# A decode-attention backward kernel: ordering the heads by batch, so that one batch's serial chain runs under the other batch's heads

## The chip, the cores and the metric

One core of one Trainium2 chip. The metric is the device time of one execution in microseconds (us); lower is better.

## The reference

A transformer block for one new token per batch (B = 2) with adaptive layer norm: attention over a cache of 8192 keys and values (32 heads of width 128), then a gated MLP. What is asked for is the output and all the gradients of its inputs. Cut to what matters:

```python
def _A_ref(x, k_cache, v_cache, wq, wo):
    q = (x @ wq).reshape(B, Sq, H, Dh).transpose(0, 2, 1, 3)
    scores = jnp.einsum('bhqd,bhkd->bhqk', q, k_cache) * Dh ** (-0.5)
    p = _softmax(scores, axis=-1)
    o = jnp.einsum('bhqk,bhkd->bhqd', p, v_cache)
    return o.transpose(0, 2, 1, 3).reshape(B, Sq, H * Dh) @ wo
...
    x = x + ga * _A_ref(h, A_k_cache, A_v_cache, A_wq, A_wo)
    h = _layernorm(x, axis=-1) * (1 + cb) + sb
    x = x + gb * _B_ref(h, B_w1, B_w3, B_w2)
...
_out, _vjp = jax.vjp(_f, A_x, A_k_cache, A_v_cache, ...)     # gradients of all of these
```

K, V, dK and dV are 134 MB each; everything else is small. Each of the 64 (batch, head) pairs has 2 MB of K and of V. The gradients dV = p dO and dK = ds q need dO, and dO comes from the end of the block back through the MLP and `wo`. So there is a serial chain between the two passes over the heads: O, attention projection, norm, MLP forward, MLP backward, norm backward, dO. **That chain mixes heads but not batches**: batch 0's chain needs the heads of batch 0 only.

## The kernel before

It has three parts, one after the other. Heads alternate between the batches. Time is cut into *slots*, eight to a head; in a slot of stage A TensorE does 8 transposes of K blocks, 8 score matmuls and 16 matmuls for M (a 128 x 128 product of V and weighted K, needed for dq) and for one more column.

```python
    def hb(i):
        return i % B, i // B                 # batch, head: the batches alternate
    ...
    def load(store, src, i):                 # 2 MB of K or V into one of ten "big" tiles
    ...
    # stage A: scores, softmax, M; 64 heads
    for t in range(NSLOT + MOFF + 1):
        i, g = divmod(t, NG)
        ...
        kts[(i, g)] = transposes(K[i], g, g in (2, 6))
        ...
                nc.tensor.matmul(S_ps[si][:, cc:cc + 1], kt[:, j, :], qT_bf[:, h, b:b + 1], ...)
        ...
            mm_m(mi, mg)                     # 16 matmuls, N = 129 and N = 1
            if mg == NG - 1:
                if mi < NHD - KEEPV: V.pop(mi)          # the last two V heads are kept
                if mi + 4 < NHD:     load(K, A_k_cache, mi + 4)
                if mi + 3 < NHD:     load(V, A_v_cache, mi + 3)
                if mi == min(2, NHD - 5): load_wo()
                if mi == NHD - 3:         load_ffn()
    # the middle: one long dependent sequence for both batches, with the weights
    # transposed on TensorE for the backward products
    ...
        for h in range(H):
            nc.tensor.matmul(av[:, dc, :], wo_v[h // (H // 2)][:, h % (H // 2), dc * P:(dc + 1) * P],
                             O_bf[:, h, :], start=(h == 0), stop=(h == H - 1))
    for a in range(2):
        for h0 in range(0, H, 4):
            t_wo(a, h0)                      # transposes of wo; later of w2, w1, w3
    ...                                      # MLP forward and backward, dO
    # stage C: V again, dV and dK; 64 heads; small outputs as "tasks" in between
    for t in range(NSLOT + LAG + 2 * NQ + 4):
        ...
            kts[(n, g)] = transposes(V[order[n]], g, g in (2, 6))
        ...
            ev_dv(n, g // 2)                 # VectorE outer product, 128 x 2048, into a big tile; 1 MB stores
        ...
            ev_dk(u // NG, (u % NG) // 2)
```

Of the kernel before, what the change touches and what calls it, by code (L numbers as in the profile page):

```python
# [18 lines left out]
def kernel(  # L19
# [48 lines left out]
    NBIG = 10  # L68
# [4 lines left out]
    def hb(i):  # L73
        return i % B, i // B
# [8 lines left out]
    ktp = ctx.enter_context(tc.tile_pool(name="ktp", bufs=5))  # L83
# [6 lines left out]
    def big():  # L90
        return bigp.tile([P, BIG], BF16, name="big", tag="big")

# [15 lines left out]
    E2 = cst.tile([P, NHD, KK, 2], BF16, name="E2")  # L108
# [31 lines left out]
    V = {}  # L140

    def load(store, src, i):
        b, h = hb(i)
        t = big()
        v = t[:, 0:KK * P].rearrange("p (k d) -> p k d", k=KK)
        qd.dma_start(v, src[b, h].rearrange("(p kk) d -> p kk d", p=P))
        store[i] = v
# [10 lines left out]
    load(K, A_k_cache, 0)  # L158
    load_wq(1)
    load(K, A_k_cache, 1)  # L160
    load_wq(2)
    load_wq(3)
    for a in range(2):
        qd.dma_start(wm_v[a][:, :, M1:MD], wm_d[:, 2 * a:2 * a + 2, M1:MD])
    load(V, A_v_cache, 0)
    load(K, A_k_cache, 2)
    load(V, A_v_cache, 1)
    load(K, A_k_cache, 3)
# [114 lines left out]
    evac_n = [0]  # L283

    def evac(dst, src):
        if evac_n[0] % 2 == 0:
            nc.scalar.copy(dst, src)
        else:
            nc.vector.tensor_copy(dst, src)
        evac_n[0] += 1  # L290

    S_ps = {}
    M_ps = {}
    ek = {}
    kts = {}
    M_t = {}
    MOFF = NG + LAG + 5
    NSLOT = NHD * NG

    def pair(ap, n):  # L300
        return ap.rearrange("p k (a b) -> p k a b", b=2)

    def transposes(src, g, dve):
        tp = tps.tile([P, GRP, P], BF16, name="tp", tag="tp")
        for j in range(GRP):
            nc.tensor.transpose(tp[:, j, :], src[:, g * GRP + j, :], identb[:])  # L306
        kt = ktp.tile([P, GRP, P], BF16, name="kt", tag="kt")
        if dve:
            nc.vector.tensor_copy(kt[:], tp[:])  # L309
        else:  # L310
            nc.scalar.copy(kt[:], tp[:])  # L311
        return kt

    def chain_rowmax(i):
        rm = hw.tile([P, 1], BF16, name="rm", tag="rm")
        nc.vector.tensor_reduce(rm[:], S_ps[i][:, 0:KK], AX.X, ALU.max)
        kts[("rm", i)] = rm

    def chain_b(i):
        s = S_ps[i]  # L320
        nc.tensor.matmul(s[:, P:2 * P], kts.pop(("rm", i))[:].to_broadcast((P, P)), nident[:],  # L321
                         start=True, stop=True)
        nm = hw.tile([P, 1], F32, name="nm", tag="nm")
        nc.vector.tensor_reduce(nm[:], s[:, P:2 * P], AX.X, ALU.min)  # L324
        kts[("nm", i)] = nm

    def chain_e(i):
        s = S_ps.pop(i)
        nc.scalar.activation(E2[:, i, :, :], s[:, 0:KK].unsqueeze(2).to_broadcast((P, KK, 2)), ACT.Exp,  # L329
                             bias=kts.pop(("nm", i))[:], scale=SCL, accum_out=rsum[:, i:i + 1])  # L330

    def scale_k(i, q):
        t = ekp.tile([P, QK, 130], BF16, name="ek", tag="ek")
        ks = slice(q * QK, (q + 1) * QK)
        nc.vector.tensor_tensor(pair(t[:, :, 0:P], QK), pair(K[i][:, ks, :], QK),  # L335
                                E2[:, i, ks, :].unsqueeze(2).to_broadcast((P, QK, P // 2, 2)), ALU.mult)
        nc.gpsimd.tensor_copy(t[:, :, P:P + 1], E2[:, i, ks, 0:1])  # L337
        ek[(i, q)] = t

    def mm_m(i, g):  # L340
# [3 lines left out]
        t = ek[(i, g // 2)]  # L344
        for j in range(GRP):
            kk = g * GRP + j
            nc.tensor.matmul(m[:, 0:P + 1], V[i][:, kk, :], t[:, kk % QK, 0:P + 1],  # L347
                             start=(kk == 0), stop=(kk == KK - 1), skip_group_check=True)
            nc.tensor.matmul(m[:, P + 1:P + 2], K[i][:, kk, :], E2[:, i, kk, 0:1],  # L349
                             start=False, stop=(kk == KK - 1), skip_group_check=True)  # L350
        if g == NG - 1:
            K.pop(i)

    def m_evac(i):
        m = M_ps.pop(i)
        nc.scalar.copy(M_all[:, i, :], m[:, 0:P])  # L356
        nc.vector.tensor_copy(OK[:, i, :], m[:, P:P + 2])  # L357

    KEEPV = 2
    extra = {}  # L360

    def at(slot, f):
        extra.setdefault(slot, []).append(f)

    for pc in range(1, NPC):
        at(2 * pc, lambda pc=pc: q_part(pc))
    at(NG, lambda: mod_part(2 * NC, MC))
# [3 lines left out]
    def load_wo():  # L371
        for a in range(2):
            t = big()
            v = t[:, 0:H // 2 * D].rearrange("p (h d) -> p h d", d=D)
            qd.dma_start(v, A_wo.rearrange("(h p) d -> p h d", p=P)[:, a * (H // 2):(a + 1) * (H // 2), :])
            wo_v.append(v)

    wn = {}
    nfull = F // P

    def load_ffn():
        for nm, ap in (("w1", B_w1), ("w3", B_w3)):
            t = big()
            wn[nm] = t[:, 0:NC * F].rearrange("p (k f) -> p k f", k=NC)
            qd.dma_start(wn[nm], ap.rearrange("(k p) f -> p k f", p=P))
        t = big()
        wn["w2"] = t[:, 0:FC * D].rearrange("p (k d) -> p k d", k=FC)
        qd.dma_start(wn["w2"][:, :nfull, :], B_w2[0:nfull * P].rearrange("(k p) d -> p k d", p=P))
        if FL != P:
            qd.dma_start(wn["w2"][:FL, nfull, :], B_w2[nfull * P:F])  # L390

    M_all = None
    Mt = None
    for t in range(NSLOT + MOFF + 1):
        i, g = divmod(t, NG)
        u = t - (NG + LAG + 2)
        if u >= 0 and u % NG == 0 and u // NG < NHD:
            chain_e(u // NG)
        if i < NHD:
            if g == 0:  # L400
                S_ps[i] = stps()
            kts[(i, g)] = transposes(K[i], g, g in (2, 6))
        for f in extra.pop(t, []):
            f()
        s = t - LAG
        if 0 <= s < NSLOT:
            si, sg = divmod(s, NG)
            b, h = hb(si)
            kt = kts.pop((si, sg))
            for j in range(GRP):  # L410
                cc = sg * GRP + j
                nc.tensor.matmul(S_ps[si][:, cc:cc + 1], kt[:, j, :], qT_bf[:, h, b:b + 1],  # L412
                                 start=True, stop=True)
        for off, f in ((0, chain_rowmax), (1, chain_b)):
            u = t - (NG + LAG + off)
            if u >= 0 and u % NG == 0 and u // NG < NHD:
                f(u // NG)
        u = t - (NG + LAG + 3)
        if u >= 0 and u % 2 == 0 and u // NG < NHD:
            scale_k(u // NG, (u % NG) // 2)  # L420
        u = t - MOFF
        if 0 <= u < NSLOT:
            mi, mg = divmod(u, NG)
            mm_m(mi, mg)
            if mg == NG - 1:
                if mi < NHD - KEEPV:
                    V.pop(mi)
                if mi + 4 < NHD:
                    load(K, A_k_cache, mi + 4)
                if mi + 3 < NHD:  # L430
                    load(V, A_v_cache, mi + 3)
                if mi == min(2, NHD - 5):
                    load_wo()
                if mi == NHD - 3:
                    load_ffn()
        if t == NG:
            load(V, A_v_cache, 2)
        u = t - MOFF - 1
        if u >= 0 and u % NG == NG - 1:
            if M_all is None:  # L440
                Mt = big()
                M_all = Mt[:, 0:NHD * P].rearrange("p (i d) -> p i d", d=P)
            m_evac(u // NG)

    woT = [big(), big()]
    woT_v = [t[:, 0:2 * HD].rearrange("p (k m) -> p k m", k=2) for t in woT]

    def tgroup(blocks, dsts):
        tp = tps.tile([P, GRP, P], BF16, name="tp", tag="tp")
        flat = tp[:].rearrange("p a b -> p (a b)")  # L450
        for o, n, src, rows in blocks:
            nc.tensor.transpose(flat[:n, o:o + rows], src, identb[:rows, :rows])
        for dst, (n, o, w, k) in dsts:
            s = flat[:n, o:o + w]
            if k > 1:
                s = s.rearrange("p (k m) -> p k m", k=k)
            evac(dst, s)

    def t_wo(a, h0):
        nh = min(4, H - h0)  # L460
        blocks = []
        for d2 in range(2):
            for hh in range(nh):
                h = h0 + hh
                src = wo_v[h // (H // 2)][:, h % (H // 2), (2 * a + d2) * P:(2 * a + d2 + 1) * P]
                blocks.append(((d2 * nh + hh) * P, P, src, P))
        tgroup(blocks, [(woT_v[a][:, :, h0 * P:(h0 + nh) * P], (P, 0, 2 * nh * P, 2))])

    tot = mtps()
    nc.tensor.matmul(tot[:, 0:NHD], onesf[:], rsum[:], start=True, stop=True)  # L470
    rtot = col("rtot", H)
    rtot_f = rtot[:].rearrange("p h b -> p (h b)")
    nc.vector.tensor_scalar(rtot_f, tot[:, 0:NHD], 0.5, None, ALU.mult)
    nc.vector.reciprocal(rtot_f, rtot_f)
    O32 = col("O32", H)
    O32_f = O32[:].rearrange("p h b -> p (h b)")
# [528 lines left out]
```

## Time and profile before

1856.85 us was the median of four runs (1851.69 to 1862.42). The profiled execution has a span of 1847.5 us.

| stage | from, us | to, us | what binds it |
|---|---|---|---|
| A | 40 | 768 (last M matmul) | TensorE |
| middle | 768 | 822 (first dV store issued) | the dependent sequence; no large transfer |
| C | 822 | 1823 (last store issued) | DMA |

First the part of the profile's page that shows the span in 40 slices of 46 us. Digits are tenths of a slice in which the engine was busy; PEclk is the TensorE clock granted, in tenths of full speed.

```profile
PE   5889999999999999888868776676555555555560
PEclk9999999999999999976555558576766565656665
DMA  9998999999999999449999999999999999999996
GB/s 389 412 374 326 383 394 380 388 379 380 380 372 367 371 361 361 186 179 387 415 411 420 416 415 423 418 418 417 421 419 417 418 418 417 416 415 413 416 415 254
```

The hole is at slices 17 and 18. Left of it, from slice 5 on, DMA moves 361 to 394 GB/s; right of it, from slice 20 to the last but one, 411 to 423: stage A could take more bytes, stage C could not. Busy time by stretches says why. The columns are the stretch and its length, busy time and count for five engines, the granted clock, the DMA engines' busy share and GB/s.

```profile
core 0: us, PE busy (x) PEld busy (x) DVE busy (x) ACT busy (x) POOL busy (x), PEclk, DMA share, GB/s
185.00:277.00 92.00, 89.52 (x2167) 88.63 (x2164) 54.72 (x77) 55.62 (x77) 16.48 (x33) 1.00 0.98 389
462.00:554.00 92.00, 86.28 (x2084) 85.43 (x2082) 52.34 (x75) 53.17 (x73) 19.07 (x32) 1.00 0.94 376
760.00:780.00 20.00, 18.28 (x418) 18.02 (x415) 10.83 (x18) 6.04 (x10) 3.15 (x4) 0.91 0.30 104
780.00:800.00 20.00, 13.76 (x279) 13.25 (x277) 8.13 (x35) 9.38 (x15) 0.00 (x0) 0.74 0.01 2
900.00:1000.00 100.00, 76.52 (x782) 57.11 (x780) 62.74 (x71) 53.45 (x81) 21.23 (x38) 0.50 1.01 413
```

TensorE is busy 97% of the first of these stretches of A and 94% of the second, at full clock. In C the clock is halved for most of the time (0.50 from 900 to 1000 us) and nobody minds, because DMA's share is 1.01. The ends of the hole come from the first and last start of one line's instructions: the M matmul, and the store of a dV or dK half.

```profile
L347 PE MATMUL m_ps<-ek,big x4096: 217/217/269, 43.7 to 767.9; 128*128 128x129 bf16 x196
L903 POOL DMA_DIRECT2D out_dram<-big x256: 531/531/676, 822.1 to 1823.3; - x128
```

### The profile page before, as it was taken

The numbers are of one execution on the slowest core, as the hardware profiler recorded it, in microseconds if no ns is written. First come the engines' busy times: TensorE is split into PE (matmuls) and PEld (weight loads), VectorE is DVE, ScalarE is ACT, GpSimd is POOL, SyncE is SP. The second block draws the span as 40 slices with busy tenths as digits, with TensorE's granted clock in tenths as the row PEclk, the third lists the DMA queues.
The fourth block names the chain that finished last, engine by engine and source line by source line (L and its number), as shares of the span: only waits on it lengthen the run. The fifth ranks groups of instructions, "written<-read, shape, count | busy, mean of one in ns | idle before, by whom it ended". The sixth has DMA issues, their size and how long they took to land. (4 is left out here: it accounts for less than half of the span.)

```text
span 1847.5 us, 58876 instructions
## 1 busy us (share of the span) xinstructions
PE 1387.5 (75%) x26588; PEld 1293.8 (70%) x26588; DVE 1132.5 (61%) x1415; ACT 955.3 (52%) x1244; POOL 303.9 (16%) x557
## 2 busy tenths in 40 slices
PE   5889999999999999888868776676555555555560
PEld 5889999999999998876556565575455555555550
DVE  2545565655555555547656666677687666666682
ACT  3545565565555555447546566474444444444440
POOL 0111111222222211102211111211111111111111
PEclk9999999999999999976555558576766565656665
DMA  9998999999999999449999999999999999999996
GB/s 389 412 374 326 383 394 380 388 379 380 380 372 367 371 361 361 186 179 387 415 411 420 416 415 423 418 418 417 421 419 417 418 418 417 416 415 413 416 415 254
DMA packets 79784, 709.57 MB, mean 384 GB/s; under 512 B 8160, under 2 KB 13644, under 8 KB 21932
## 3 DMA queue, kind: packets, MB, share of 16 engines
q1 hardware_dynamic: 38304, 421.57, 56.9%
q0 software_dynamic: 41216, 284.22, 37.0%
q8 instruction: 208, 3.41, 0.7%
q14 instruction: 44, 0.36, 0.0%
q10 hardware_dynamic: 12, 0.01, 0.0%
HBM read 421.57 MB, written 284.20 MB: 382 GB/s over the span
## 5 line engine op out<-in xcount | busy, mean ns | idle before, releaser
L311 ACT COPY kt<-tp 128x1024 bf16<-128x1024 bf16 x768 | 776.3, 1014 | 677.5 <-PE tp L306 667.9
L306 PE MATMUL tp<-identb,big 128*128 128x128 bf16 x8192 | 798.6, 256 | 26.3 <-issue 14.5
L306 PEld LDWEIGHTS <-big 128*128 128x128 bf16 x8192 | 601.2, 115 | 118.7 <-issue 111.4
L347 PE MATMUL m_ps<-ek,big 128*128 128x129 bf16 x4096 | 409.9, 218 | 10.4 <-issue 10.0
L958 PE MATMUL s_ps<-DO_bf,kt 128*128 128x1 bf16 x4096 | 196.4, 169 | 263.5 <-DVE kt L309 262.3
L958 PEld LDWEIGHTS <-kt 128*128 128x128 bf16 x4096 | 192.9, 111 | 282.6 <-DVE kt L309 280.9
L349 PE MATMUL m_ps<-E,big 128*128 128x1 bf16 x4096 | 381.5, 165 | 9.1 <-issue 8.6
L895 DVE TENSOR_TENSOR big<-QD,E 128x2048 bf16<-128x2048 bf16 x256 | 311.4, 1217 | 117.0 <-DMA out_dram<-big 67.5
L895 DVE TENSOR_TENSOR big<-QD,ds 128x2048 bf16<-128x2048 bf16 x256 | 311.8, 1219 | 95.4 <-PE tp L306 62.8
L309 DVE COPY kt<-tp 128x1024 bf16<-128x1024 bf16 x256 | 176.1, 688 | 300.4 <-PE tp L306 256.3
L347 PEld LDWEIGHTS <-big 128*128 128x128 bf16 x4096 | 345.0, 96 | 10.7 <-issue 10.0
L349 PEld LDWEIGHTS <-big 128*128 128x128 bf16 x4096 | 343.4, 96 | 11.7 <-issue 11.4
L335 DVE TENSOR_TENSOR ek<-big,E 128x2048 bf16<-128x2048 bf16 x256 | 306.5, 1218 | 2.5 <-ACT E L329 2.2
L903 POOL DMA_DIRECT2D out_dram<-big x256 | 136.3, 532 | 831.8 <-DVE big L895 355.8
L337 POOL COPY ek<-E 128x16 bf16<-128x16 bf16 x256 | 143.7, 563 | 619.9 <-ACT E L329 272.3
L412 PE MATMUL s_ps<-qT_bf,kt 128*128 128x1 bf16 x4096 | 177.9, 164 | 14.5 <-issue 11.3
L412 PEld LDWEIGHTS <-kt 128*128 128x128 bf16 x4096 | 158.3, 97 | 18.8 <-issue 14.3
L710 ACT CAST stg<-m_ps 128x512 bf16<-128x512 f32 (+2 forms) x123 | 71.5, 591 | 106.2 <-DMA out_dram<-stg 69.8
L709 PE MATMUL m_ps<-big 2*128 2x512 bf16 (+2 forms) x123 | 71.2, 579 | 33.4 <-ACT stg L710 32.7
L324 DVE TENSOR_REDUCE nm<-s_ps 128x1 f32<-128x128 f32 x64 | 18.6, 291 | 58.4 <-PE s_ps L321 58.4
L357 DVE COPY OK<-m_ps 128x2 f32<-128x2 f32 x64 | 10.2, 159 | 55.4 <-ACT big L356 55.4
L814 ACT COPY kt<-tp 128x1024 bf16<-128x1024 bf16 x28 | 28.7, 1044 | 3.5 <-PE tp L811 3.3
(198 smaller groups left out, 481.9 us busy)
## 6 DMA issues: line engine op xcount, KB each, us to landing
out_dram<-big POOLq DMA_DIRECT2D x256, 1024.0 KB, 29.5
big<-in_A_v_cache_dram SPq DMA_DIRECT2D x126, 2048.0 KB, 13.3
big<-in_A_k_cache_dram SPq DMA_DIRECT2D x64, 2048.0 KB, 8.7
out_dram<-stg POOLq DMA_DIRECT2D x22, 512.0 KB, 19.5
big<-in_A_wq_dram SPq DMA_DIRECT2D x8, 512.0 KB, 14.5
big<-in_A_wo_dram SPq DMA_DIRECT2D x2, 2048.0 KB, 17.8
big<-in_A_wq_dram SPq DMA_DIRECT2D x2, 2048.0 KB, 15.2
big<-in_w_mod_dram SPq DMA_DIRECT2D x2, 1536.0 KB
```

Source lines behind the costliest of these rows:

```text
L306: nc.tensor.transpose(tp[:, j, :], src[:, g * GRP + j, :], identb[:])
L309: nc.vector.tensor_copy(kt[:], tp[:])
L311: nc.scalar.copy(kt[:], tp[:])
L335: nc.vector.tensor_tensor(pair(t[:, :, 0:P], QK), pair(K[i][:, ks, :], QK), E2[:, i, ks, :].unsqueeze(2).to_broadcast((P, QK, P // 2, 2)), ...
L337: nc.gpsimd.tensor_copy(t[:, :, P:P + 1], E2[:, i, ks, 0:1])
L347: nc.tensor.matmul(m[:, 0:P + 1], V[i][:, kk, :], t[:, kk % QK, 0:P + 1], start=(kk == 0), stop=(kk == KK - 1), skip_group_check=True)
L349: nc.tensor.matmul(m[:, P + 1:P + 2], K[i][:, kk, :], E2[:, i, kk, 0:1], start=False, stop=(kk == KK - 1), skip_group_check=True)
L412: nc.tensor.matmul(S_ps[si][:, cc:cc + 1], kt[:, j, :], qT_bf[:, h, b:b + 1], start=True, stop=True)
L710: nc.scalar.copy(st["t"][:lw, o:o + rw], ps[:lw, 0:rw])
L895: nc.vector.tensor_tensor(pair(dst[:, ks, :], QK), QD[n][:, which, :].rearrange("p (a b) -> p a b", b=2).unsqueeze(1).to_broadcast((P, QK, ...
L903: sq_.dma_start(dst_dram[b, h].rearrange("(p kk) d -> p kk d", p=P)[:, ks, :], t[:, ks, :])
L958: nc.tensor.matmul(DP[sn][:, cc:cc + 1], kt[:, j, :], DO_bf[:, h, b:b + 1], start=True, stop=True)
```

## The change

Its intent: heads are ordered batch by batch. Batch 0's chain is cut into small steps of one or two slots each, 165 slots in all, and laid between the slots of stage A of batch 1; batch 1's chain is laid in stage C of batch 0; C starts at slot 518, before A's last M (slot 526). So that a chain's steps are small, the backward products no longer transpose the weights on TensorE: a vector is spread over the partitions, and VectorE takes dot products of it with the rows of the weights. The chains hold `wo`, `w1`, `w3`, `w2` in four of the big tiles for most of the time, so the buffers are cut anew: seven big tiles and seven halves instead of ten big ones; K and the outputs use halves; the exponentials are stored once, not in pairs; no V head is kept from A to C (4.2 MB more to read). And there are 70 padding matmuls at slot 320. The diff, cut to its core:

```diff
-    NBIG = 10
+    NBIG = 7
+    NHALF = 7
...
     def hb(i):
-        return i % B, i // B
+        return i // H, i % H
...
+    def dot(acc, w, vec):
+        n = w.shape[-1]
+        r = w.shape[0]
+        junk = tps.tile([P, GRP * P // 2], F32, name="junk", tag="tp")
+        nc.vector.scalar_tensor_tensor(junk[:r, 0:n], w, 1.0, vec, ALU.mult, ALU.mult,
+                                       accum_out=acc)
...
+        def attn_pe(dc):
+            hold[dc] = scr(1)
+            for h in range(H):
+                nc.tensor.matmul(hold[dc], wo_v[h // (H // 2)][:, h % (H // 2), dc * P:(dc + 1) * P],
+                                 O_bf[:, b, h:h + 1], start=(h == 0), stop=(h == H - 1))
...
+    CS0 = end_a(sA[H - 1]) + 1
+    FS0 = max(NG + 4, CS0 - 2 * length(dh[0]))
+    want(FS0 - 2, "big", 1, lambda: load_ffn(0))
+    want(FS0 - 1, "big", 1, lambda: load_ffn(1))
+    t0 = lay(dh[0], FS0)
+    t0 = lay(dh[1], t0 + 1)
+    t0 = max(CS0, t0 + 1)
+    want(t0 - 2, "big", 1, lambda: load_wo(0))
+    want(t0 - 1, "big", 1, lambda: load_wo(1))
+    t0 = lay(ch[0], t0)
+    TC = max(NG * NHD + 6, t0 + 1)
+    CS1 = end_a(sA[NHD - 1]) + 1
+
+    def pad_pe():
+        d = scr(1)
+        for _ in range(70):
+            nc.tensor.matmul(d, identb[:], identb[:, 0:1], start=True, stop=True)
+
+    at(320, PL_X, pad_pe)
+    t1 = lay(ch[1], max(CS1, t0 + 1))
+    sC = [TC + NG * n for n in range(H)]
...                                 # removed: the middle, with its 260 weight transposes
```

`want(slot, ...)` queues a load in the order of the slot in which its data is needed; `lay` puts a chain's steps into slots.

## The prediction

> **What bounds the kernel now**, read from busy time by stretches and instruction groups by line.
> - Stage A (40 to 768 us, scores and M for 64 heads) is TensorE's: PE is busy 96% between 185 and 554 us at a granted clock of 1.00, while DMA moves about 380 GB/s. DMA showed 423 GB/s at 45 to 85 us, when reads really bind, so A has some 10% of DMA in hand. A head takes 10.95 us early, 11.4 late.
> - The middle (attention projection, MLP forward and backward, dO) is serial. The last M matmul starts at 768 us, the first dV product at 818, its store is issued at 822. The slices there show 186 and 179 GB/s; from 755 to 845 us about 15.5 MB move where 417 GB/s would move 37.5: some 53 us of DMA are lost.
> - Stage C (822 us to the end) is DMA's: share 1.01, 413 to 419 GB/s, 6.29 MB and so 15.1 us a head. The chain of waits ends in stores. Trainium skill, "DMA: Bandwidth & Descriptors", "Where 436 GB/s comes from": the ports' ceiling is 435 GB/s; the trace's 417 to 425 agrees, so C itself can't get faster.
>
> **What the change does.** It orders heads by batch. Batch 0's chain runs inside A of batch 1, batch 1's inside C of batch 0; C starts at slot 518, before A's last M (slot 526). Weight transposes (260 matmuls, 20 us busy) and their 34 evictions become about 78 DVE dot products per batch.
> - Removed: nearly the whole hole. First dV store moves from 822 to about 779 us.
> - Added to A: about 260 thin matmuls of batch 0 (128 took 3.5 us, so 7 us), 34 spreads (2 us), 70 padding matmuls (2 us), small waits: 12 to 17 us, on the critical path, since PE binds. The wo load leaves the start, where PE lost some 18 us, but wo and MLP weights (8.4 MB, 20 us of DMA) now come in mid A, with V down to two buffers: about even.
> - Added to C: two V heads are no longer kept, 4.2 MB or 10 us. DVE: a head needs 8 products of 1.22, two copies of 0.69 and one of 0.34 us, 11.5 us; a 512-wide dot is estimated at 0.69 us (from the 128-wide reduction at 0.29 and 64-wide vector operations at 0.225), 67 over 20 heads, plus small steps: 14.2 of 15.1 us. Tight; about 5 us of DMA may leak.
>
> Sum on the profile: 779 + 1001 (C as before, first to last store issue) + 10 + 5 + 22 us of drain = 1817; less loss in A brings about 1808. Against 1847.5 that is -1.6 to -2.1%. Predicted time **1815 us**, range 1785 to 1846. Chances: faster by over 2% 0.54, within 2% 0.43, slower 0.03.
>
> **What would show it.** The two slices near 180 GB/s are gone, none below 300 between first and last; the first dV store issues at 770 to 785 us; A stays PE-bound at 96%; C stays at DMA share 1.0 and 410 to 418 GB/s; traffic 714 MB; DVE busy over 85% while batch 1's chain runs.
>
> **What would make it wrong.** (1) Slower: with two V buffers and blocked-at-the-head loads, A starves around slots 216 to 290 and PE idles long enough to drop its clock (Trainium skill, "TensorE: Matmul & The Clock Gate", "The HAM clock gate": idle windows halve the clock; the trace shows 0.66-0.71 after such gaps at 135 and 165 us). (2) DVE becomes C's limit while batch 1's chain runs: DMA below 400 GB/s there. (3) Faster: A's thin matmuls fit into its issue gaps, and the early PE loss vanishes: A ends by 770, total about 1795.

## The result

1832.46 us, median of 11 runs (1822.54 to 1835.92), against 1854.62 us for the kernel before (15 runs, 1846.14 to 1862.42). Ratios are the mean time of one kernel's runs over that of the other's of the same rounds, so not quite the ratio of the medians. Here it is 0.9869, 95% interval 0.9849 to 0.9889: 1.3% faster, clear of noise, and less than 2%. The profiled execution has a span of 1824.1 us.

The slices after:

```profile
PE   5988999898999999986555657776868667455463
PEclk9999999998999999976565556555565856666676
DMA  9988999999889999999999999999999999999997
GB/s 387 374 318 347 383 376 402 408 371 331 354 349 379 383 371 374 370 355 391 421 418 421 423 423 412 422 408 407 409 415 414 423 415 411 422 418 402 415 412 315
```

The hole has gone. But slices 10 to 12 have sunk to 331 to 354 GB/s, which they did not before. The ends of the stages, from the same two kinds of line:

```profile
L434 PE MATMUL m_ps<-ek,big x4096: 217/217/272, 43.7 to 795.3; 128*128 128x129 bf16 x196
L909 POOL DMA_DIRECT2D out_dram<-half x256: 531/531/676, 788.0 to 1808.8; - x128
```

| | before | after | difference |
|---|---|---|---|
| first store issued | 822.1 | 788.0 | -34.1 |
| first to last store issued | 1001.2 | 1020.8 | +19.6 |
| last store issued to the end | 24.2 | 15.3 | -8.9 |
| span | 1847.5 | 1824.1 | -23.4 |

A's last M comes 27.4 us later than before. Where those went is read from the steps of the heads. I take the start of each head's second reduction of the softmax maximum, one per head, which stands in both kernels. Heads are counted from 0, in us:

| | head 25 | head 40 | head 63 | heads 25 to 40 | a head after 40 |
|---|---|---|---|---|---|
| before | 330.6 | 497.1 | 759.9 | 166.5 | 11.43 |
| after | 325.6 | 523.0 | 780.6 | 197.4 | 11.20 |

The changed kernel is 5 us ahead at head 25, loses 31 us up to head 40, where batch 0's chain and its weights come in, and is a little faster per head after that: at head 63 it is 21 us behind. The other 7 us come between that head and the last M, where C's first slots are already mixed in. Within heads 25 to 40, heads 32 to 36 take 61.5 us against 45.3. Busy time in 2-us stretches shows the worst of it:

```profile
426.00:428.00 2.00, 1.48 (x35) 1.35 (x34) 1.12 (x2) 1.32 (x3) 0.00 (x0) 1.00 1.07 440
428.00:430.00 2.00, 0.00 (x1) 0.01 (x1) 1.90 (x6) 0.05 (x1) 0.37 (x2) 1.00 1.02 426
430.00:432.00 2.00, 2.00 (x59) 2.00 (x60) 0.39 (x1) 1.01 (x1) 0.26 (x1) 0.92 0.98 414
432.00:434.00 2.00, 2.00 (x39) 2.00 (x37) 0.16 (x1) 0.75 (x1) 0.00 (x0) 0.50 0.99 414
438.00:440.00 2.00, 2.00 (x39) 2.00 (x37) 0.07 (x1) 0.78 (x1) 0.18 (x1) 0.50 0.94 250
444.00:446.00 2.00, 2.00 (x38) 2.00 (x37) 0.58 (x5) 1.01 (x1) 0.22 (x1) 0.67 0.98 414
446.00:448.00 2.00, 2.00 (x52) 2.00 (x49) 0.82 (x2) 0.15 (x1) 0.00 (x0) 1.00 0.32 127
```

TensorE stops at 428; the list of waits in 425 to 432 us names K:

```profile
PE tp L373 <- DMA half<-in_A_k_cache_dram: 2.5, 1, 2.5
```

Then the granted clock (third number from the right) is 0.50 from 432 to about 445 us, and the number of matmuls in 2 us falls from 52-60 to 39. The K was late because the two halves of `wo` (4 MB) had been queued ahead of it at 406 us. At the same place 128 thin matmuls (one moving column each) of the attention projection are inserted, 32 to a slot. A page of the Trainium skill, "TensorE: Matmul & The Clock Gate", section "The HAM clock gate", says that an idle window of about 3.4 us halves the clock; here 2.5 us without a matmul (0.52 us before 428 and the 2 us after it) and the thin stretch after it were enough. Which of the two did it the trace alone does not say. It is also not the only dip: between heads 25 and 40 the clock is 0.50 for 27 us in all, from 342.9 to 349.7 us after another late K (2.3 us), from 418.0 to 421.4 after a stop of 1.7 us with no wait behind it, and from 506.8 to 510.2.

Stage C shows a second loss, at its start, and the VectorE load that I had worried about:

```profile
780.00:800.00 20.00, 17.16 (x393) 16.56 (x390) 15.90 (x19) 11.52 (x20) 6.80 (x8) 1.00 0.99 380
800.00:820.00 20.00, 15.67 (x295) 15.16 (x295) 15.59 (x30) 9.13 (x13) 2.12 (x4) 0.51 0.87 356
820.00:840.00 20.00, 15.83 (x316) 15.59 (x315) 16.97 (x36) 11.19 (x19) 3.19 (x6) 0.55 0.92 352
900.00:1000.00 100.00, 53.39 (x788) 51.38 (x786) 75.78 (x109) 41.13 (x60) 13.29 (x25) 0.59 1.01 421
1000.00:1100.00 100.00, 57.79 (x806) 56.33 (x806) 79.85 (x117) 40.55 (x56) 12.75 (x24) 0.50 1.01 421
```

While batch 1's chain runs, VectorE is busy 76 to 80% and DMA moves 421 GB/s. Between 800 and 840 us it moves 352 to 356.

My theory at this point: (B) the weights arrive in two bursts that make K late, and TensorE's stop then halves its clock. Rivals: (P) the chain's own TensorE work, one for one, since TensorE binds A; (V) two V buffers instead of three starve A; (C) batch 1's chain disturbs the start of C.

### The profile page after: what moved, and what is told of

The parts are those of the page before. It is cut to its first block, busy times and chain, and to the rows that moved or that the text cites. A ratio compares the mean times of both kernels' runs of the same rounds, so it can differ in the third digit from the quotient of the medians.

```text
span 1824.1 us, 59234 instructions
## 1 busy us (share of the span) xinstructions
PE 1373.8 (75%) x26464; PEld 1277.8 (70%) x26464; DVE 1211.8 (66%) x1714; ACT 965.7 (53%) x1387; POOL 369.6 (20%) x621
## 3 DMA queue, kind: packets, MB, share of 16 engines
q8 instruction: 207, 3.39, 0.7%
## 4 chain that ended last, share of the span: by engine, by line
issue 31%; DMA 19%; PE 7%; POOL 5%; DVE 1%; POOLq 0%; ACT 0%; ACTq 0%
DMA out_dram<-half 13%; POOL out_dram L909 5%; DMA out_dram<-stg 4%; PE tp L373 3%; PE m_ps L434 3%; DMA half<-in_A_k_cache_dram 1%; DVE half L904 1%; PE s_ps L393 1%; DMA big<-in_A_v_cache_dram 0%; PE s_ps L646 0%; PE m_ps L1024 0%; PE s_ps L881 0%; POOLq L909 0%; DVE kt L376 0%; PE m_ps L436 0%
## 5 line engine op out<-in xcount | busy, mean ns | idle before, releaser
L373 PE MATMUL tp<-identb,big 128*128 128x128 bf16 x3968 | 456.0, 286 | 105.4 <-DVE junk L598 103.1
L373 PEld LDWEIGHTS <-big 128*128 128x128 bf16 x3968 | 351.7, 130 | 210.6 <-issue 201.5
L434 PE MATMUL m_ps<-ek,big 128*128 128x129 bf16 x4096 | 412.3, 218 | 8.9 <-issue 7.7
L904 DVE TENSOR_TENSOR half<-DOr,e 128x2048 bf16<-128x2048 bf16 x256 | 311.5, 1217 | 160.5 <-DMA out_dram<-half 155.5
L436 PE MATMUL m_ps<-e,half 128*128 128x1 bf16 x4096 | 384.3, 165 | 8.8 <-issue 8.8
L434 PEld LDWEIGHTS <-big 128*128 128x128 bf16 x4096 | 347.6, 97 | 8.6 <-issue 7.9
L436 PEld LDWEIGHTS <-half 128*128 128x128 bf16 x4096 | 344.6, 96 | 11.0 <-issue 10.8
L373 PE MATMUL tp<-identb,half 128*128 128x128 bf16 x4224 | 334.8, 223 | 23.0 <-issue 12.7
L904 DVE TENSOR_TENSOR half<-Qr,ds 128x2048 bf16<-128x2048 bf16 x256 | 311.8, 1219 | 42.5 <-DMA out_dram<-half 41.0
L419 DVE TENSOR_TENSOR ek<-half,e 128x2048 bf16<-128x2048 bf16 x256 | 309.1, 1220 | 2.6 <-ACT e L411 2.3
L909 POOL DMA_DIRECT2D out_dram<-half x256 | 136.3, 532 | 775.5 <-DVE half L904 594.0
L421 POOL COPY ek<-e 128x16 bf16<-128x16 bf16 x256 | 155.5, 608 | 576.0 <-ACT e L411 299.4
L373 PEld LDWEIGHTS <-half 128*128 128x128 bf16 x4224 | 251.6, 99 | 27.3 <-issue 19.0
L393 PE MATMUL s_ps<-qT_bf,kt 128*128 128x1 bf16 x4096 | 178.2, 164 | 12.0 <-issue 8.7
L393 PEld LDWEIGHTS <-kt 128*128 128x128 bf16 x4096 | 159.4, 97 | 15.7 <-issue 13.6
## 6 DMA issues: line engine op xcount, KB each, us to landing
big<-in_A_v_cache_dram SPq DMA_DIRECT2D x126, 2048.0 KB, 12.2
```

What stands on the lines that cost most here:

```text
L373: nc.tensor.transpose(tp[:, j, :], block(j), identb[:])
L393: nc.tensor.matmul(S_ps[i][:, cc:cc + 1], kt[:, j, :], qT_bf[:, h, b:b + 1], start=True, stop=True)
L419: nc.vector.tensor_tensor(pair(t[:, :, 0:P]), pair(K[(i, hf)][:, o:o + QK, :]), E2[i][:, ks, :].unsqueeze(2).to_broadcast((P, QK, P // 2, ...
L421: nc.gpsimd.tensor_copy(t[:, :, P:P + 1], E2[i][:, ks, 0:1])
L434: nc.tensor.matmul(m[:, 0:P + 1], vb_(V[i], kk), t[:, kk % QK, 0:P + 1], start=(kk == 0), stop=(kk == KK - 1), skip_group_check=True)
L436: nc.tensor.matmul(m[:, P + 1:P + 2], kb_(K, i, kk), E2[i][:, kk, 0:1], start=False, stop=(kk == KK - 1), skip_group_check=True)
```

## The experiments

Programs that are equal up to slot 320 (head 39) reached head 25 at 315.9 to 327.1 us, so a single trace's stage A is good to some 5 us; differences below that are taken from the timed rounds or not at all.

### 1. No padding

```diff
-    at(320, PL_X, pad_pe)
```

> The 70 padding matmuls at slot 320 are taken out. Theory P (every TensorE instruction put into stage A lengthens it one for one): 70 x 27 ns = 2 us shorter, 1830 us against 1832. Theory B (the loss in A comes from the weight loads arriving in two bursts): no change beyond 2 us either; this run only fixes the zero point for the run with 770. If it moves by over 4 us, the padding does something other than take time.

Measured: 1852.75 us (4 runs, 1847.8 to 1858.77), ratio to the kernel before 0.9992 (0.9953 to 1.0031). Taking out 2 us of do-nothing work costs 20 us, the whole gain of the change. So the padding is not padding. In the trace nothing differs up to head 40 (523.2 us, against 523.0), but heads after 40 take 12.24 us instead of 11.20. Neither theory P nor theory B foresaw that; the last clause of the expectation ("does something other than take time") is what happened.

Where the time is lost is seen in the order of time on TensorE's weight loads. The bracket is the idle time before the instruction and what ended it; "issue" means nothing that the profile shows. The run without padding:

```profile
652.79 0.10 PEld L434 LDWEIGHTS <-big 128*128 128x128 bf16 x1 [0.74 <-issue]
659.28 0.10 PEld L436 LDWEIGHTS <-half 128*128 128x128 bf16 x1 [1.22 <-issue]
665.32 0.10 PEld L434 LDWEIGHTS <-big 128*128 128x128 bf16 x1 [0.81 <-issue]
671.53 0.10 PEld L436 LDWEIGHTS <-half 128*128 128x128 bf16 x1 [0.95 <-issue]
677.57 0.10 PEld L436 LDWEIGHTS <-half 128*128 128x128 bf16 x1 [0.79 <-issue]
```

The changed kernel with its 70:

```profile
664.84 0.10 PEld L393 LDWEIGHTS <-kt 128*128 128x128 bf16 x1 [0.48 <-issue]
671.06 0.12 PEld L393 LDWEIGHTS <-kt 128*128 128x128 bf16 x2 [0.91 <-issue]
682.12 0.20 PEld L393 LDWEIGHTS <-kt 128*128 128x128 bf16 x5 [0.36 <-issue]
687.88 0.21 PEld L393 LDWEIGHTS <-kt 128*128 128x128 bf16 x6 [0.50 <-issue]
693.82 0.24 PEld L393 LDWEIGHTS <-kt 128*128 128x128 bf16 x7 [0.67 <-issue]
```

A gap comes every 6 us, twice a head, at other places of the slot in the two kernels (L434 and L436 are the M matmuls, L393 the scores). From 520 to 770 us there are 41 such gaps, with 33 us, without the padding, and 22, with 12 us, with it (gaps over 0.15 us on the weight loads that wait for nothing). A slot's TensorE work is the same for all slots, so something with a period of half a head makes them. A page of the Trainium skill, "Runtime: NRT & Kernel Launch", section "Instruction fetch mechanics", says that an engine's instructions are refilled in blocks of 16 KiB, 256 instructions. The trace agrees in amount: 2 x 26,464 TensorE instructions at 64 bytes are 3.39 MB, and the profile's instruction queue shows 3.39 MB in 207 packets, 16.4 KB each. A head is 514 TensorE instructions and a few of the chain, so two refills.

The kept traces also show it in time. They hold each packet of the instruction queue. Of the 41 gaps without the padding 39 end 1.1 to 1.7 us after such a packet has landed (median 1.4), of the 22 with it 18, and in the kernel before 29 of 29, although the stretch from 1.1 to 1.7 us after a packet is only about a tenth of the time. So nearly all of these gaps are TensorE waiting for its next block of instructions. A packet takes 0.97 us on average without the padding and 1.00 with it: it is not a slower transfer that makes the gaps longer.

### 2. 770 padding matmuls

```diff
-        for _ in range(70):
+        for _ in range(770):
```

> 770 padding matmuls instead of 70, in one go at slot 320, in stage A of batch 1: 700 x 27 ns = 19 us more TensorE work, no more bytes. Theory P (stage A is bound by TensorE, so thin matmuls add one for one): last M matmul 19 us later and 1851 us in all. Rival (stage A has slack in its lead of loaded K and V, so the added work is partly made up by faster heads afterwards): under 12 us, below 1844 us.

Measured: 1875.83 us (1870.88 to 1885.94), ratio 1.0122. Against 1832 that is 43 us for 700 matmuls, too much for either theory. Against the run *without* padding, in the same rounds, it is 23 us for 770, 30 ns each, and its heads after 40 take 12.12 us, like those without padding. Head 39, with the padding in it, takes 38.3 us against 12.2. So theory P holds, thin matmuls add to A one for one, and on top of it the refill phase is the bad one again: 770 matmuls are 1540 instructions, four more than six blocks of 256.

### 3. The weights' loads earlier and apart

```diff
-    want(FS0 - 2, "big", 1, lambda: load_ffn(0))
-    want(FS0 - 1, "big", 1, lambda: load_ffn(1))
+    want(72, "big", 1, lambda: load_ffn(0))
+    want(120, "big", 1, lambda: load_ffn(1))
...
-    want(t0 - 2, "big", 1, lambda: load_wo(0))
+    want(168, "big", 1, lambda: load_wo(0))
```

> The same loads of the MLP and output weights, but three of the four are asked for earlier and far apart (slots 72, 120, 168; the fourth, half of wo, stays at slot 273), so that each 2 to 2.7 MB has five or six heads to be absorbed. Bytes and TensorE work are the same. Theory B (bursts: K comes late at 341 and 430 us, PE stops 2.5 us, its clock is then gated to half for some 14 us): those waits and the clock dip between 415 and 446 us go or shrink, heads 26 to 39 take 11.2 us each, A's last M comes 15 to 20 us earlier (775 to 780 us) and the time is 1812 to 1820 us. Theory P (the chain's own TensorE work): no change, 1828 to 1836 us.

Measured: 1826.34 us (1820.56 to 1832.32), ratio 0.9853 (0.9806 to 0.9901), an interval that holds the changed kernel's 0.9869. The expected 12 to 20 us did not come: in the trace no K is late between heads 25 and 40, and still the clock is 0.50 from 427 to 441 us and heads 32 to 36 take 59.0 us. Theory B alone falls.

### 4. The fourth load early too, so two V buffers from head 25 on

```diff
-    want(t0 - 1, "big", 1, lambda: load_wo(1))
+    want(200, "big", 1, lambda: load_wo(1))
```

> As the spaced run, with the fourth load (half of wo) early too, at slot 200, so that V has two buffers instead of three from about head 25 on. If two V buffers starve stage A by themselves, heads after 25 get slower than 11.4 us and the time rises by 10 us or more over the spaced run. If only the burst counts, it is equal to the spaced run or up to 5 us faster, since the last burst at 405 us is gone too.

Measured: 1825.93 us (1820.33 to 1831.76), ratio 0.9847 (0.9807 to 0.9886), as the run before it. Heads after 40 take 11.29 us, and TensorE never waits for a V load in stage A of this trace. Two V buffers do not starve A; theory V is out. Heads 25 to 40 take 14 us less than in the changed kernel (183.6 against 197.4), but head 25 comes 17 us later (342.2 against 325.6), with more refill gaps and a halved clock for 24 us before it, against 3; why they fell there is not shown. Heads 32 to 36 take 57.5 us, and here is why B fell. In 3-us stretches, and one of 4 us:

```profile
426.00:429.00 3.00, 3.00 (x77) 3.00 (x73) 1.90 (x4) 2.50 (x4) 1.06 (x1) 1.00 0.86 330
432.00:435.00 3.00, 2.16 (x63) 2.09 (x63) 2.33 (x6) 1.10 (x3) 1.30 (x3) 1.00 1.00 418
435.00:438.00 3.00, 3.00 (x69) 3.00 (x67) 0.16 (x1) 1.01 (x1) 0.00 (x0) 0.52 0.49 202
441.00:444.00 3.00, 2.68 (x63) 2.62 (x61) 0.22 (x2) 1.18 (x2) 0.00 (x0) 0.50 0.84 350
447.00:450.00 3.00, 3.00 (x53) 3.00 (x52) 0.82 (x2) 0.90 (x1) 0.00 (x0) 0.70 0.58 243
457.00:461.00 4.00, 4.00 (x131) 4.00 (x128) 2.44 (x7) 1.65 (x3) 0.74 (x1) 1.00 0.95 360
```

No K is late in this run (the waits of TensorE in 425 to 452 us add up to 1.1 us, on small steps), TensorE counts as busy but for pauses of 0.5, 0.3 and 0.3 us (at 432, 434 and 442), and the clock is still halved from 435 to 449 us; the 128 thin matmuls go in from 433 to 444. New theory H: slots with 32 one-column matmuls in them leave the array so little active that its clock is halved; a late K does it as well. The last line sets a limit to H: from 457 to 461 us the MLP puts 44 one-column matmuls in each of two slots, with no pause, and the clock stays at 1.00 (as it does for the same bursts in the changed kernel). So a burst alone is not enough; the short pauses around it, or its place in the clock's records, which change in steps of 3.41 us, must count too.

### 5. 198 padding matmuls

```diff
-        for _ in range(70):
+        for _ in range(198):
```

> The runs with 0 and 770 padding matmuls both had heads of 12.3 us after slot 320 against 11.2 us with 70, with TensorE gaps of 0.6 to 1.2 us twice a head for which nothing is waited for. 3.39 MB of instruction traffic in 207 packets is 16.4 KB a packet, 256 TensorE instructions at 64 bytes, so I estimate a refill twice a head. A padding matmul is two instructions: 770 is 4 instructions off six whole periods (as 0), 70 is 140 off, about half a period. Theory R (where in the head the refill falls sets how much of it shows): 198 = 70 + 128 matmuls shift by one more whole period and so keep heads of 11.2 us; A's last M 3.5 us later (799 us), time 1833 to 1839 us. Rival N (70 is a lucky number, or any other number is bad): heads of 12.3 us, 1853 to 1860 us.

Measured: 1834.64 us (1826.68 to 1839.01), ratio 0.9916 (0.9885 to 0.9948); heads after 40 take 11.34 us, with 25 gaps without a wait and 15 us from 520 to 770. Within the expected range, and 20 us away from the rival's. Together with the run of 770 this fits an effect that repeats with 128 matmuls, 256 instructions: 0 and 770 are bad, 70 and 198 are good (a period of 512 would fit these four as well; 256 is the size of a packet). Why more of a refill shows at one phase than at another is not settled; half a head is also the rhythm in which K loads are issued, but the packets themselves take the same time at both phases (run 1).

### 6. The thin matmuls spread over more slots

```diff
-            def f(dc=dc):
-                if dc > 0:
-                    attn_ev(dc - 1)
-                attn_pe(dc)                       # 32 matmuls in a slot
-            put(1, f)
+            for q in range(4):
+                def f(dc=dc, q=q):
+                    if dc > 0 and q == 0:
+                        attn_ev(dc - 1)
+                    attn_pe(dc, q)                # 8 in a slot
+                put(1, f)
...                                               # w1, w3: 44 in a slot to 12; w2: 44 to 11
```

> The thin matmuls of the chains (attention projection 32 in a slot, MLP projections 44 in a slot) are spread to 8, 12 and 11 in a slot; number of instructions, loads and results are the same. The spaced runs showed that the loss at heads 33 to 35 stays without any late K: the clock falls to 0.5 while the 128 thin matmuls are inserted. Theory H (32 one-column matmuls in a slot leave the array so little active that its clock is halved for some 13 us): the clock stays at 1.00 between slots 274 and 320 but for the late K, heads 33 to 35 take 12 us each instead of 21, 14, 12, A ends 8 to 12 us earlier, time 1820 to 1825 us. Rival (their own run time or their waits on VectorE cost it): spread over more slots they cost the same, 1829 to 1836 us.

Measured: 1825.32 us (1820.07 to 1827.93), ratio 0.9854 (0.9825 to 0.9884), and a **wrong result** in two outputs (relative error 0.21 in d_c and d_w_mod). It fits what the Trainium skill's "PSUM — Partial Sum Buffer" says in "The four PSUM rules": the first matmul of a group clears the written flags of the whole bank, and a running sum in another column is then overwritten. My attention sum ran over four slots in the bank in which score matmuls start anew in each slot. The trace counts as many TensorE instructions as that of the changed kernel, so I still use the time. In the trace a K is late at 428 us for 2.6 us, since the loads were left as they were, and the clock is 0.50 from 433 to 450 us with only 8 thin matmuls in a slot; heads 32 to 36 take 57.4 us. So a late K is also enough by itself. Each of the runs 4 and 6 took away one of two causes and left the other; H is not decided by run 6.

### 7. The kernel before with 64 padding matmuls

```diff
+        if t == 320:
+            for _ in range(64):
+                nc.tensor.matmul(S_ps[i][:, 2 * P:2 * P + 1], identb[:], identb[:, 0:1], start=True, stop=True)
```

> The kernel before, with 64 padding matmuls at its slot 320: 2 us of work and a shift of half a refill period for heads 40 to 63, which take 11.5 us there against 10.9 us before. If theory R holds for that kernel too and its phase is a bad one, heads 40 to 63 go to about 11.0 us and the time falls by 8 to 12 us (0.5%); then part of the measured gain of the change is not due to the overlap at all. If before is at a good phase by chance, it gets slower by up to 20 us. If the effect belongs to the changed kernel only: +2 us.

Measured: 1861.18 us (1850.39 to 1867.68), ratio to the kernel before 1.0046 (1.0003 to 1.0089): the interval just clears 1, and alone does not show more than the 2 us of the matmuls. In the trace heads after 40 take 11.85 us instead of 11.43, 10 us over 23 heads, and the refill gaps from 520 to 770 us add up to 26 us instead of 20. The kernel before has the same sensitivity, and stands at a better phase than this one.

### 8. Batch 1's chain 40 slots later

```diff
-    t1 = lay(ch[1], max(CS1, t0 + 1))
+    t1 = lay(ch[1], max(CS1, t0 + 1) + 40)
```

> Batch 1's chain starts 40 slots later in stage C; everything before slot 527 is the same. Between 780 and 860 us DMA moves only 352 to 380 GB/s, some 9 us short of 420. Theory C (the chain's start takes VectorE and TensorE from the first heads of C, which have to fill the store queue): with the chain later, 800 to 840 us shows 400 GB/s or more and the time falls by 4 to 8 us. Rival (the first heads of C are slow because few half tiles are free and the tail of A still runs): no change, 1829 to 1836 us.

Measured: 1823.99 us (1813.39 to 1829.62), ratio 0.9844 (0.9803 to 0.9886). The start of C, which was 356 and 352 GB/s:

```profile
800.00:820.00 20.00, 14.34 (x227) 13.56 (x225) 19.93 (x22) 11.23 (x17) 3.73 (x7) 0.59 1.00 396
820.00:840.00 20.00, 12.63 (x186) 11.84 (x184) 12.23 (x13) 10.30 (x13) 2.67 (x5) 0.59 1.01 423
```

(40 + 71) GB/s over 20 us each are 2.2 MB, 5 us at 420 GB/s. Theory C holds in so far as the chain's first steps had held up the first products of C. VectorE's busy time had not: it was 15.6 and 17.0 of each 20 us in the changed kernel. But there, from 795 to 845 us, it waits for TensorE (4.2 us for transposes, 2.0 for the chain's attention sums) and ScalarE (2.2), and here only for stores to free a buffer (9.1). The time moved as expected; the interval alone would not show it, and the profiled run is the fastest of its four. The program up to slot 527 is that of the changed kernel, and yet A's last M comes at 789.5 us against 795.3: single traces differ that much.

### 9. The three edits together

```diff
-    want(FS0 - 2, "big", 1, lambda: load_ffn(0))
-    want(FS0 - 1, "big", 1, lambda: load_ffn(1))
+    for a in range(2):
+        want(64 + 40 * a, "big", 1, lambda a=a: load_ffn(a))            # a first piece
+        for q in range(1, 4):
+            want(64 + 40 * a + 10 * q, "big", 0, lambda a=a, q=q: load_ffn_q(a, q))
...                                    # wo the same, from slots 152 and 212, 12 slots apart
-                nc.tensor.matmul(hold[dc], wo_v[...][...], O_bf[:, b, h:h + 1],
-                                 start=(h == 0), stop=(h == H - 1))
+                nc.tensor.matmul(hold[dc][:, q:q + 1], wo_v[...][...], O_bf[:, b, h:h + 1],
+                                 start=(h % (H // 4) == 0), stop=(h % (H // 4) == H // 4 - 1))
...                                    # a column for each quarter, summed on VectorE; spread as in 6
-    t1 = lay(ch[1], max(CS1, t0 + 1))
+    t1 = lay(ch[1], max(CS1, t0 + 1) + 40)
```

> Three edits together: the weights of the MLP and of the output projection come in sixteen pieces of 0.3 to 0.7 MB, ten to twenty slots apart (no late K); the thin matmuls of the chains are spread to 8, 12 and 11 in a slot, with partial sums in columns of their own (so the result should be right this time); batch 1's chain starts 40 slots later in C. Padding and number of TensorE instructions are as in the changed kernel, so the refill phase is kept. Theory H + B (the clock dips at heads 33 to 35 when either a late K or a burst of thin matmuls leaves the array idle, and each of the single edits left the other cause in place): the clock stays at 1.00 from 410 to 450 us, heads 33 to 35 take 12 us each, A's last M at 775 to 782 us, C at 400 GB/s or more from 800 us on, time 1803 to 1813 us. Rival (the single edits' gains were the spread between runs): 1824 to 1834 us and the dip still there.

Measured: 1817.05 us (6 runs, 1812.89 to 1821.23), right result, ratio 0.9802 (0.9775 to 0.9828). That beats both kernels; its slowest run is faster than the changed kernel's fastest. Whether it is over 2% faster than the kernel before stays unclear. Run 8, which has the late chain alone, stands at 0.9844 (0.9803 to 0.9886), and the two intervals overlap: what the two edits in A are worth in time is not clear of noise. It missed the expected 1803 to 1813. The stretch where the clock had been halved:

```profile
428.00:430.00 2.00, 2.00 (x59) 2.00 (x57) 0.80 (x4) 1.39 (x3) 0.67 (x1) 1.00 0.86 246
432.00:434.00 2.00, 2.00 (x58) 2.00 (x55) 0.82 (x2) 0.31 (x1) 0.00 (x0) 1.00 0.98 414
438.00:440.00 2.00, 2.00 (x57) 2.00 (x55) 0.51 (x2) 1.04 (x2) 0.59 (x1) 1.00 0.58 234
444.00:446.00 2.00, 2.00 (x56) 2.00 (x54) 1.34 (x2) 1.51 (x2) 0.71 (x1) 1.00 0.95 401
446.00:448.00 2.00, 0.47 (x15) 0.41 (x13) 0.00 (x0) 0.41 (x1) 0.00 (x0) 1.00 0.97 406
```

The clock stays at 1.00 from 404 to 496 us, even over a gap of 1.5 us at 446. With both causes out the dip is out; with either one in (runs 3 and 4, and 6) it is there, as it is in all the other traces with the thin matmuls 32 to a slot. That decides for H and B together, as far as the one trace of this run goes. Heads 32 to 36 take 51.6 us, 10 less, though not the 45.3 of the kernel before; 3.5 of these 6 us are the time of the 128 thin matmuls at 27 ns. A's last M comes at 786.2 us (795.3 in the changed kernel) and the first store at 778.9 (788.0); from first to last store C takes 1014.8 us (1020.8).

### 10. Every dot product of batch 1's chain twice

```diff
-        nc.vector.scalar_tensor_tensor(junk[:r, 0:n], w, 1.0, vec, ALU.mult, ALU.mult, accum_out=acc)
+        for _ in range(2 if now[0] > TC else 1):
+            nc.vector.scalar_tensor_tensor(junk[:r, 0:n], w, 1.0, vec, ALU.mult, ALU.mult, accum_out=acc)
```

> In the changed kernel every dot product of batch 1's chain is issued twice in stage C (56 more, 0.69 + 0.13 us each: 46 us more VectorE work between about 840 and 1112 us; the sums are the same). VectorE is busy 76 to 84% there. Theory D (VectorE has slack in C, DMA binds): DMA stays at 415 GB/s or more, VectorE goes to 90 to 95%, time within 3 us of 1832. Rival (the prediction's step: VectorE is at the edge in C and DMA leaks): doubling it pushes DMA below 400 GB/s there and costs 10 to 30 us.

Measured: 1831.72 us (1824.95 to 1841.74), ratio 0.9884 (0.984 to 0.9929), the same as the changed kernel within the interval.

```profile
900.00:1000.00 100.00, 54.80 (x775) 52.54 (x772) 83.64 (x133) 40.95 (x61) 12.75 (x24) 0.53 1.01 423
1000.00:1100.00 100.00, 57.56 (x810) 56.04 (x808) 99.15 (x169) 40.66 (x55) 12.75 (x24) 0.50 1.01 415
```

VectorE goes to 84 and 99% and DMA stays at 415 to 423 GB/s. The chain's dots take 276 us from first to last in both kernels, so VectorE had room for another 46 us there. It was not quite free: in the trace C takes 1027.2 us from first to last store against 1020.8, with 306 GB/s from 800 to 820 us; the timed runs are too far apart to show 6 us.

### 11. C waits for batch 1's chain

```diff
-    TC = max(NG * NHD + 6, t0 + 1)
     CS1 = end_a(sA[NHD - 1]) + 1
+    TC = max(CS1, t0 + 1) + length(ch[1]) + 1
```

> The overlap with C is undone: stage C starts only after batch 1's chain has ended; batch 0's chain stays inside A. The bare chain of some 165 slots has no other work: 56 dots of 0.83 us, 32 evictions and some 40 small steps each behind another engine. Theory: it takes 80 to 120 us alone, far more than the 48 us hole of the kernel before for both batches, so time 1910 to 1950 us with slices of a few GB/s; the dot form of the chain pays only as filler under transfers. Rival (the dots are as fast as the transposed form): 50 us or less, 1880 us.

Measured: 1880.48 us (2 runs, 1876.13 and 1884.83), ratio 1.0144; about 48 us more than the changed kernel (the profiled run is the slower of the two). The hole is back:

```profile
800.00:820.00 20.00, 8.50 (x209) 7.60 (x208) 9.18 (x44) 3.28 (x7) 0.00 (x0) 0.50 0.12 50
820.00:840.00 20.00, 3.40 (x20) 2.17 (x19) 12.36 (x46) 3.81 (x13) 0.00 (x0) 0.50 0.48 177
840.00:860.00 20.00, 0.00 (x0) 0.00 (x0) 20.00 (x63) 0.18 (x1) 0.00 (x0) 0.50 0.36 139
```

The last M starts at 796.2 us and the first store is issued at 868.9: one batch's chain, bare, takes 73 us, against 54 for both batches in the kernel before. My 80 to 120 us was too long. The time landed on the rival's figure for another reason: with the chain out of it, and the first V heads loaded during the hole, C took 997 us instead of 1021, which gives 24 of the 81 us back by which the first store comes later. As a piece of work the dot form is much slower than the transposed one; under transfers in C it costs little.

### 12. The kernel before with 96 padding matmuls

The edit of run 7 with 96.

> The kernel before with 96 padding matmuls at slot 320, three quarters of an estimated refill period (64 gave +12 us, of which 2 us are the padding's own time). What is open: whether the kernel before, as it stands, is at a bad phase from which padding alone would bring much of the change's 1.3%. If its phase is near the best, 96 gives 1853 to 1865 us (2.6 us of own time and no faster heads); if a better one exists here, heads 40 to 63 go from 11.5 to 11.2 us or less and the time to 1845 us or below.

Measured: 1845.15 us (1833.66 to 1852.34), ratio to the kernel before 0.9949 (0.9898 to 0.9999). Heads after 40 take 11.04 us, and their refill gaps from 520 to 770 us add up to 14 us instead of 20. The kernel before could have had some 0.5% from padding alone; the interval barely excludes nothing at all, and the profiled run, the second slowest of four, has the same span as the kernel before.

## Why the prediction was right or wrong

The time, 1832 us, lies in the range (1785 to 1846), and the mechanism is the one predicted: the hole goes, A gets longer, C gets longer. The prediction leaned to over 2% (0.54), and it was 1.3%. Point by point:

- **The hole goes: right.** First store at 788 us, predicted 770 to 785, so 3 us late. Run 11, which brings the hole back for batch 1's chain, costs 48 us.
- **"12 to 17 us" added to A, and the weight loads "about even": wrong in size.** This is the term of the sum that was off. A's last M came 27 us later; heads 25 to 40 took 31 us longer than before, of which earlier and later heads gave 10 back. Counted in the two traces, these 15 heads hold 355 more matmuls, 11 us at 30 ns; that term was sized right (27 ns assumed, 30 ns in run 2). What was left out: 6 us of waits, 5 of them for late K's; 4 us more of refill gaps; and a granted clock of 0.50 for 27 us, against none before. The 10 us that remain are about what the clock explains: 39 instead of some 58 matmuls in 2 us, over 27 us, is an estimated 9 us. The prediction had named the late K and the clock as a risk, (1), but put no time on it, and did not see that the thin matmuls can do it without a late K (runs 3 and 4). Runs 4, 6 and 9 show both causes.
- **C, 1016 us from first to last store: right to 5 us (1020.8), for a partly wrong reason.** "Tight; about 5 us of DMA may leak" to VectorE fails. A dot takes 0.82 us (0.69 + 0.13 for reading the sum out), more than the 0.69 estimated, but 11 of the 67 counted are not in C, VectorE was busy 76 to 80% and not over 85, and doubling the dots changed the time by less than the runs can tell (run 10: C 6 us longer in the trace, for 46 us of work). The leak is real and sits elsewhere: at the start of C, where the chain's first steps hold up C's products (run 8).
- **The drain, 22 us: 15 measured** (17 in all the other traces of the changed program). The halves in flight at the end are fewer; that was not tested.
- **Traffic 714 MB, DMA share 1.0 in C, no slice under 300 GB/s: right.** A at 96% busy is right only up to 277 us (95.5%); 370 to 462 us has 90%.
- **1815 us after a sum of 1817 on the profile** was a slip of its own: the median of the timed runs is 7 to 8 us above the profiled span in both kernels, so the sum said about 1825, and 1815 only with the "less loss in A" that did not come.
- **What the prediction did not have at all: the refill phase.** The 70 padding matmuls were costed as 2 us of work. They are worth 20. Without them the change as a whole gains nothing (0.9992), and its 1852.75 us would have been outside the range: that the number landed inside is luck in this respect. The kernel before gains some 0.5% from padding of its own. Of the three phases tried in the kernel before (0, 64, 96) and the two in the changed kernel, the best stand at 0.9949 and 0.9869, the worst at 1.0046 and 0.9992. Like for like the overlap is worth an estimated 0.5 to 0.8% (0.9992/1.0046 and 0.9869/0.9949), and the rest of the 1.3% is phase. With the intervals of the four ratios each of these is uncertain by about 0.6%, the smaller one not clear of zero; the rounds were on different chips and few phases were tried. So this is a size, not a figure.

Where the 53 us of the hole went, on the profiles: the last M of A came 27 us later and C's stores took 20 us longer, of which 10 us were the V heads no longer kept (4.2 MB at 417 GB/s) and about 5 us the disturbed start. A few us of either remain unassigned.

## What to carry to other kernels

Moving a serial chain under a stage is worth the hole only minus what the host stage's own limit charges for it: count the chain's work on the engine that binds the stage, spread both its loads and its thin instructions so that neither lets the host's engine fall idle, and put it where the stage is bound by something else (here DMA in C, where doubling its dots cost less than the noise). When an unrolled TensorE-bound loop changes in length, measure it at two or three paddings before crediting the change: a difference of 1% can be where the instruction refills fall. If two causes are each sufficient, removing one shows nothing; remove both.

## What the Trainium skill lacked or had wrong

- "Runtime: NRT & Kernel Launch", "Instruction fetch mechanics" says that crossing a 16 KiB boundary is "mostly hidden". In a stage with TensorE 88 to 96% busy and DMA at 346 to 376 GB/s (520 to 770 us, without and with the padding) it was not: gaps of 0.2 to 1.9 us with no wait behind them, up to twice a head, 12 to 33 us in 250 us, nearly all of them ending 1.1 to 1.7 us after an instruction packet has landed, and 20 us of kernel time depending on the phase (0 and 770 padding matmuls bad, 70 and 198 good, which fits a period of 256 instructions).
- "TensorE: Matmul & The Clock Gate", "The HAM clock gate", speaks of idle windows of about 3.4 us. A later section, on PSUM-queue cycling, tells of a clock that oscillates from short idle times between groups of matmuls, without their length. Here single stops shorter than 3.4 us did it: in stage A of the 14 traces (55 to 760 us), all 14 stops of TensorE over 2 us that began at full clock (four of them over 3.4 us) were followed within 3.6 us by a clock of 0.50, 24 of the 37 between 1.5 and 2 us (1.7 us at 415 us in the changed kernel was, 1.5 us at 446 us in run 9 was not), and 15 of the 68 between 1.2 and 1.5 us. No page gives a number for one-column matmuls: with no late data and pauses of 0.5 and 0.3 us, four slots with 32 of them each went with 0.50 for 14 us (run 4); 8 in a slot did not (run 9), nor did 44 in each of two slots (run 4).
- "DMA: Bandwidth & Descriptors", "Where 436 GB/s comes from" agrees: the highest rates held over 100 us were 421 to 424 GB/s under its ceiling of 435. Its statement that about 358 GB/s binds for traffic between HBM and SBUF does not hold here: slices 20 to 39 of the changed kernel show 402 to 423, with this one core running. The section itself gives a measurement of 425.
- "PSUM — Partial Sum Buffer", "The four PSUM rules" agrees with the failure of run 6 (error 0.21) and with its cure in run 9, groups that are closed before another starts in the bank.
